# A spectral mixer and SwiGLU kernel: x loaded ahead of the filter, imaginary filter products first, and a later start for part of the second block

## The chip, the cores and the metric

The kernel runs on one core of one Trainium2 chip. A core has TensorE (PE, matmuls into PSUM; its weight loads are listed as PEld), VectorE (DVE), ScalarE (ACT), GpSimd (POOL) and SyncE (SP), which here issues transfers only. SP and POOL each issue DMA transfers into a queue of their own (q1 for SP, q0 for POOL in the profile); 16 DMA engines carry both. The metric is device time in microseconds, lower is better.

## The reference

The input x has 8 batches of 3008 rows of 256 channels. Each batch is filtered along its rows by a product in the frequency domain; then every row goes through an RMS norm and a gated feed-forward layer.

```
X = np.fft.rfft(x, axis=1)                     # x: (8, 3008, 256)
Y = X * (filt_r + 1j * filt_i)[None, :, :]     # filter: (1505, 256)
y = np.fft.irfft(Y, n=3008, axis=1).reshape(24064, 256)
rms = np.sqrt(np.mean(y * y, axis=-1, keepdims=True) + 1e-06)
xn = y / rms * rms_g
g = xn @ w_gate                                # (256, 1536)
out = (g / (1 + np.exp(-g)) * (xn @ w_val)) @ w_out   # (1536, 256)
```

## The kernel before

A batch is called a block. Its Fourier transform of length 3008 = 47 x 64 is done in two steps by matrix tables. `wa` transforms over 64 points, `wb` over 47 (with twiddles, one 96-column table for each of 32 values k2), `wi` and `wai` go back. All four tables, and two identity matrices (`ident` in fp16, `idf` in fp32) for turning tiles on PE, come from constants in HBM. Activations are kept in fp16, PSUM sums in fp32.

The steps of a block, with the function and its line in the profile:

- `x_load` (L188): a block's x comes in four groups (`xc`, 393 KB each as written), issued by POOL, which casts to fp16.
- `a0_unit` (L359) for block 0, `a_unit` (L208) for the others: the 64-point step on PE, then a copy from PSUM by ACT or DVE. Block 0 is turned on PE (`tr0_unit`, L369) with eight DVE copies into the tiles `t2`. The other blocks write `t1` to HBM (`z_store`, L213) and read it back turned (`t2_load`, L223).
- `b_unit` (L243) and `s_part` (L233 for e = 0, L236 for e = 1): the 47-point step for four k2 and one half of the channels; 16 units a block. From one PSUM bank DVE makes two products with the filter table `ff`: e = 0 with the real part, e = 1 with the negated and plain imaginary part. In block 0 both are summed and turned on PE (`yt0_unit`, L420).
- `bi_unit` (L287): back over 47 points; the result is copied into `uu`.
- `t4_load` (L301): SP turns `uu` by four DMA transposes into `t4`. In block 0, `t4_first` (L436) turns the first four row groups on PE, so that they need not wait for the DMA.
- norm: `first_norm` (L448 to L472) and `n_first`, `q_unit`, `scale_split`, `scale_apply` (L485 to L526) make `xn` for the first two row groups of block 0; `n_unit` and its followers make the rest.
- feed-forward: `gv` (L548 on PE, Silu at L552 on ACT, product at L553 on DVE) and `down` (L565). A block has 6 row groups m of 12 column tiles jt; each (m, jt) is a slot, 576 slots in all.

The filter: `f_load` (L384) brings filter rows in fp32, in six quarters of 512 KB (three row pieces i, f = 0 imaginary, f = 1 real), `f_unit` (L391) turns one with four PE transposes, and ACT writes it with two copies into `ff`. `f_neg` (L411) on POOL writes the negated imaginary part, `f_last` (L407) two edge columns.

The weights: `w_load` (L596) stages w_gate and w_val in fp32, `w_gain` (L608) on POOL multiplies by the gain of the norm, and `wo_load` (L600) brings w_out in three thirds of four jt each.

The order is written out by hand up to the first slot, and each engine runs its instructions in that order. `fill` (L428) issues matmuls whose result nobody reads. In the front, SP issues `idf`, the first imaginary quarter, `wa`, `ident`, `wai` and three single rows; POOL issues block 0's four x groups, five filter quarters, `wb` in halves, `wi`, the staged weights, and later block 1's x. A POOL DMA reuses one of eight semaphores and so waits for the DMA that used it eight issues earlier.

After that a planner gives each unit of later blocks a slot: `at(slot, fn, ...)` fixes one, `fit` looks for the first slot whose PSUM bank (M or B) is free and where ACT or DVE have room. `a_plan`, `b_plan` and `norm_plan` use it. In slot i PE gets `gv(i)`, then the planned units, then `down(i - 2)`.

Of the kernel before, what the change touches and what calls it, by code (L numbers as in the profile page):

```python
# [10 lines left out]
FP32 = mybir.dt.float32  # L11
FP16 = mybir.dt.float16
# [8 lines left out]
P = 128  # L21
D = 256
B = 8
# [15 lines left out]
def _make_tables():  # L39
    n2 = np.arange(N2)  # L40
    wa = np.zeros((P, P))
    wai = np.zeros((P, P))
    for h in range(2):
        r = slice(h, P, 2)
        for k2 in range(K2):
            c = np.cos(2 * np.pi * ((n2 * k2) % N2) / N2)
            s = np.sin(2 * np.pi * ((n2 * k2) % N2) / N2)
            re = 4 * k2 + 2 * h
            wa[r, re] = c
            wai[re, r] = c * (1.0 if k2 == 0 else 2.0)  # L50
# [12 lines left out]
    for k2 in range(K2):  # L63
        for q in range(SL):
            if q < H:
                k = k2 + 64 * q
                sign = 1.0
            else:
                j = q - H + 1
                k = 64 * j - (k2 if k2 else 32)  # L70
                sign = -1.0
                if j == H and k2:
                    continue
            th = 2 * np.pi * ((n1 * k) % N) / N
            c, sn = np.cos(th), np.sin(th)
            if k == 0 or k == NF - 1:
                sn = np.zeros(N1)
            if k2:
                wb[re, k2, q] = c
                wb[im, k2, q] = sign * sn  # L80
                wb[re, k2, SL + q] = -sn
                wb[im, k2, SL + q] = sign * c
            else:
                part = re if q < H else im
                wb[part, k2, q] = c
                wb[part, k2, SL + q] = -sn
                m = 1.0 if k in (0, NF - 1) else 2.0
                wi0[q, part] = m * c
                wi0[SL + q, part] = -m * sn
    f = np.float16  # L90
    r = np.arange(KR)
    wi = np.zeros((P, K2, KR))
    wi[:KR] = wb[:KR].transpose(2, 1, 0)
    wi[:KR, 0, :] = wi0
    wi[:, :, (r % H) * NR + r // H] = wi * S_INV_B
    return (wa.astype(f), (wai * S_INV_A).astype(f), wb.astype(f), wi.astype(f), np.eye(P).astype(f),
            np.eye(P).astype(np.float32))


@with_exitstack  # L100
def kernel(
# [10 lines left out]
):  # L112
    nc = tc.nc

    wa_np, wai_np, wb_np, wi_np, id_np, if_np = _make_tables()
    wa_d = nc.inline_tensor(wa_np, name="wa_t").ap()
    wai_d = nc.inline_tensor(wai_np, name="wai_t").ap()
    wb_d = nc.inline_tensor(wb_np, name="wb_t").ap()
    wi_d = nc.inline_tensor(wi_np, name="wi_t").ap()
    id_d = nc.inline_tensor(id_np, name="id_t").ap()  # L120
    if_d = nc.inline_tensor(if_np, name="if_t").ap()

    z_d = nc.dram_tensor("z_tmp", (B, K2, KR, D), FP16, kind="Internal").ap()

# [20 lines left out]
    wa = glob.tile([P, P], FP16)  # L145
    wai = glob.tile([P, P], FP16)
    ident = glob.tile([P, P], FP16)
    idf = glob.tile([P, P], FP32)
# [13 lines left out]
    epsb = glob.tile([P, 1], FP32)  # L162
    warm = glob.tile([P, 4], FP32)
    mhalf = glob.tile([P, 4], FP32)

    st = {b: {"x": {}, "t1": {}, "t2": {}, "s": {}, "yt": {}, "t4": {}, "y": {}, "sq": {},
              "u": {}, "xn": {}} for b in range(B)}
# [21 lines left out]
        st[b]["x"][c] = t  # L189

    def bank(i, name):
        pool, tag = ((psM, "mx"), (psG, "pg"), (psV, "pv"), (psB, "mb"))[i]
        return pool.tile([P, 512], FP32, tag=tag, name=name)

    def copy(eng, out, in_, scale=None):
# [39 lines left out]
            f2 = fv[:, :, 0:2 * SL].rearrange("p k (r q) -> p k r q", r=2)  # L235
            eng.tensor_tensor(out=o, in0=ps[:, :, ::-1, :], in1=f2, op=ALU.mult)  # L236

    def b_unit(b, i, bk=3):
        g, dh = divmod(i, 2)
        ps = bank(bk, "psb")[:, 0:4 * KR]  # L240
        for k in range(4):
            kk = 4 * g + k
            nc.tensor.matmul(ps[:, ts(k, KR)], st[b]["t2"][kk // KC][:, kk % KC, ds(dh * P, P)],  # L243
                             wb[0:KR, kk, :], start=True, stop=True)
        s = [sp.tile([P, 4, KR], FP16, tag="s%d" % e, name="s%d" % e) for e in range(2)]
        st[b]["s"][i] = (ps.rearrange("p (k r q) -> p k r q", k=4, r=2), s)
        s_part(b, i, 0)

    def b_soft(b, i, v=None):
        g, dh = divmod(i, 2)  # L250
# [124 lines left out]
    fst = {}  # L375
    FR4 = 4

    def f_load(i, f, eng):
        if i not in fst:
            fst[i] = stg.tile([P, 2, FR4, D], FP32, tag="stg", name="fs")  # L380
        t = fst[i]
        row = FR4 * P * i if i < 2 else NF - 1 - FR4 * P
        for src in ((filt_i, filt_r)[f],):
            eng.dma_start(t[:, f].rearrange("p a d -> p (a d)"),  # L384
                                raw(src, row, [[FR4 * D, P], [1, FR4 * D]]))

    def f_unit(i, f, dh, e):
# [224 lines left out]
    with tc.manual_schedule():  # L612
# [2 lines left out]
        nc.scalar.activation(out=warm, in_=epsb.to_broadcast([P, 4]), func=AXT.Sqrt)  # L615
        for c in range(NXC):
            x_load(0, c)
        nc.sync.dma_start(idf, if_d)
        f_load(0, 0, nc.sync)
        nc.sync.dma_start(wa, wa_d)  # L620
        nc.sync.dma_start(ident, id_d)
        nc.sync.dma_start(wai, wai_d)
        tail = op.tile([P, 4, D], FP32, tag="o3", name="tail")
        for f, src in ((0, filt_i), (1, filt_r)):
            nc.sync.dma_start(tail[0:1, f, :], raw(src, NF - 1, [[D, 1], [1, D]]))
        nc.sync.dma_start(tail[0:2, 2, 0:P], moe_rms_g.rearrange("(a p) -> a p", p=P))
        f_load(0, 1, nc.gpsimd)
        for i in range(1, 3):
            for f in range(2):
                f_load(i, f, nc.gpsimd)  # L630
        for h in range(2):
            nc.gpsimd.dma_start(wb[:, ts(h, K2 // 2), :], wb_d[:, ts(h, K2 // 2), :])
        nc.gpsimd.dma_start(wi, wi_d)
        w_load(0)
        w_load(1)
# [10 lines left out]
                for dh in range(2):  # L646
                    a0_unit(gq, dh, E[dh], 1 + dh)

        fill(5)
        for dh in range(2):  # L650
            f_unit(0, 0, dh, "A")
        fill(2)
        a0(0)
        fill(3)
        a0(1, 2)
        psg = bank(3, "psg")
        for f in range(2):
# [3 lines left out]
        copy("V", ff.rearrange("p e k (s q) -> p e k s q", s=3)[:, :, 0, 1:3, SL - 1],  # L661
             psg[:, 0:4].rearrange("p (e s) -> p e s", e=2))
        copy("V", gsb, psg[:, 4:6])
        fill(2)
        a0(3)
        fill(4)
        a0(4, 5)
        for dh in range(2):
            f_unit(0, 1, dh, "A")
        todo = {g: (1, *divmod(g, 2)) for g in range(4)}  # L670
        todo[4], todo[6] = (2, 0, 0), (2, 1, 0)
        for g in range(8):
            tr0_unit(g, "V")
            if g in todo:
                f_unit(*todo[g], "A")
        f_unit(2, 0, 1, "A")
        f_neg(4, 4, (0,))
        f_neg(8, 8, (0,))
        f_neg(4, 4, (1,))
        f_neg(8, 8, (1,))  # L680
        UN = K2 // 2
        od = [2, 4, 3, 5, 6, 7, 0, 1] + list(range(8, UN))
        for p in range(UN + 3):
            if p < UN:
                b_unit(0, od[p], (0, 3)[p % 2])
                s_part(0, od[p], 1)
            if p == 0:
                f_unit(2, 1, 1, "A")
                f_last()
                f_neg(0, 4)  # L690
                w_load(2)
                wo_load(0)
                f_neg(16, 16)
                wo_load(1)
                wo_load(2)
                for c in range(NXC):
                    x_load(1, c)
                for q in range(3):
                    w_gain(q)
            if p < 2:  # L700
                fill(2, 2)
            if 2 <= p < UN + 1:
                yt0_unit(od[p - 2], "A", 1)
            if p == UN + 1:
                yt0_unit(UN - 1, "V", 1, slice(0, 2))
                yt0_unit(UN - 1, "A", 0, slice(2, 4))
            if 4 <= p < UN + 3:
                bi_unit(0, od[p - 4], "AV"[p == UN + 1], 2)
            if UN + 1 <= p < UN + 3:
                fill(1, 1)  # L710
        bi_unit(0, UN - 1, "V", 3, slice(0, 2))
        bi_unit(0, UN - 1, "A", 0, slice(2, 4))
        t4_first()
        fill(2)
        for c in range(NXC):
            t4_load(0, c)
        first_norm()

        items = [(b, m, jt) for b in range(B) for m in range(6) for jt in range(JT)]
# [40 lines left out]
                at(s + d, fn, b, m)  # L760
            assert s + r[-1] + 1 < 72 * b + 12 * m

        XAT = {2: (5, 8, 11, 29), 3: (47, 51, 79, 88), 4: (112, 122, 132, 142)}

        def a_plan(b, slots):
            for i in range(12):
                opts = []
                for k in "MB":
                    opts.append((k, "A", ((k, 0, 1), ("A", 0, 0.6))))
# [41 lines left out]
        for b in range(1, B):  # L811
# [74 lines left out]
```

## Time and profile before

| | |
|---|---|
| median of 3 runs | 865.69 us (865.57 to 866.22) |
| the profiled execution | 865.26 us |
| its span, first to last instruction | 863.5 us |
| granted TensorE clock | 0.999 |
| first gate matmul of slot 0 | 43.91 us |
| first gate matmul of slot 10 | 60.39 us |

The span is the time between the first and the last instruction of the core; the execution has 1.8 us more around it. Times in the timelines are counted from the start of the span. "Idle before" is the time in which the engine waited, with what released it.

### The profile page before, as it was taken

How to read it: one execution, taken by the hardware profiler on the slowest of the kernel's cores; microseconds unless marked ns; L12 is line 12 of the kernel's file. 1: busy time of each engine (PE TensorE's matmuls, PEld its weight loads, DVE VectorE, ACT ScalarE, POOL GpSimd, SP SyncE). 2: the span in 40 equal slices, each digit the busy share in tenths (PEclk: the TensorE clock that was granted, in tenths of full speed). 3: DMA queues.
4: the chain of work that ended last, by engine and by line, in shares of the span. 5: the costliest groups of instructions: out<-in, count | busy, mean ns of one | idle time of the engine just before them, and what ended most of it. 6: DMA issues, size and time to landing. Idle time of an engine off the chain costs nothing.

```text
span 863.5 us, 17023 instructions
## 1 busy us (share of the span) xinstructions
PE 852.5 (99%) x6142; PEld 533.2 (62%) x6142; DVE 556.9 (64%) x925; ACT 613.7 (71%) x1340; POOL 296.8 (34%) x344
## 2 busy tenths in 40 slices
PE   8999999999999999999999999999999999999997
PEld 6755666566665666666666666666666666665664
DVE  4857655776666666666666676667666666555554
ACT  5887787777578756887578866888567765777443
POOL 5814841453144321534034430444123430132000
PEclk9999999999999999999999999999999999999999
DMA  9996688775975566646655658433564331521101
GB/s 283 279 179 138 135 168 167 129 137 124 196 146 120 132 150 110 148 110 143 136 127 115 130 103 173 115 87 95 136 127 93 94 72 42 125 53 49 62 25 50
DMA packets 198621, 107.98 MB, mean 125 GB/s; under 512 B 158982, under 2 KB 182920, under 8 KB 198536
## 3 DMA queue, kind: packets, MB, share of 16 engines
q1 hardware_dynamic: 190040, 86.04, 44.4%
q0 software_dynamic: 8352, 20.71, 12.4%
q8 instruction: 48, 0.79, 0.4%
q14 instruction: 37, 0.30, 0.1%
q10 hardware_dynamic: 144, 0.13, 0.0%
HBM read 45.78 MB, written 35.65 MB: 94 GB/s over the span
## 4 chain that ended last, share of the span: by engine, by line
PE 95%; DMA 2%; DVE 1%; ACT 1%; SPq 0%; issue 0%
PE po L565 28%; PE pg L548 28%; PE pv L548 28%; PE psb L243 3%; PE psi L287 2%; PE psn L316 2%; PE psa L208 2%; DMA tail<-in_moe_rms_g_dram 1%; DMA t<-uu 1%; PE psy L420 1%; PE psf L391 0%; PE pst L369 0%; DVE s L233 0%; DVE s L236 0%; DVE hh L553 0%
## 5 line engine op out<-in xcount | busy, mean ns | idle before, releaser
L553 DVE TENSOR_TENSOR hh<-pv,sg 128x512 f16<-128x512 f32 (+2 forms) x578 | 391.7, 678 | 287.3 <-ACT sg L552 222.2
L552 ACT ACTIVATE sg<-pg 128x512 f16<-128x512 f32 (+2 forms) x578 | 337.8, 585 | 216.7 <-PE pg L548 212.4
L548 PE MATMUL pg<-xn,wg 128*128 128x512 f16 (+2 forms) x1156 | 337.9, 374 | 0.0
L548 PE MATMUL pv<-xn,wv 128*128 128x512 f16 (+2 forms) x1156 | 337.8, 374 | 0.0
L565 PE MATMUL po<-wo,hh 128*128 128x256 f16 x2256 | 332.6, 272 | 0.0
L565 PEld LDWEIGHTS <-hh 128*128 128x128 f16 x2256 | 213.5, 98 | 105.3 <-issue 0.6
L270 POOL TENSOR_TENSOR ss<-s,s 128x384 f16<-128x384 f16 x112 | 102.0, 911 | 273.0 <-DVE s L236 245.3
L548 PEld LDWEIGHTS <-wv 128*128 128x128 f16 x1156 | 113.0, 98 | 130.6
L548 PEld LDWEIGHTS <-wg 128*128 128x128 f16 x1156 | 111.5, 98 | 16.9 <-issue 0.2
L342 POOL TENSOR_TENSOR xt<-y,rho 128x1024 f16<-128x1024 f32 (+1 forms) x46 | 85.4, 1857 | 2.9
L324 ACT ACTIVATE junk<-y 128x256 f16<-128x256 f32 x180 | 74.3, 413 | 2.8
L233 DVE TENSOR_TENSOR s<-psb,ff 128x384 f16<-128x384 f32 x124 | 67.8, 547 | 0.0
L236 DVE TENSOR_TENSOR s<-psb,ff 128x384 f16<-128x384 f32 x124 | 67.8, 547 | 0.0
L197 ACT ACTIVATE uu<-psi 128x384 f16<-128x384 f32 (+1 forms) x127 | 61.7, 486 | 1.5 <-PE psb L243 0.5
L197 ACT ACTIVATE y<-psn 128x512 f32<-128x512 f32 (+1 forms) x95 | 55.8, 588 | 4.2
L287 PEld LDWEIGHTS <-yt 96*128 96x128 f16 x512 | 35.4, 97 | 26.7 <-issue 1.0
L334 POOL TENSOR_TENSOR rho<-u,mhalf 128x4 f32<-128x4 f32 (+1 forms) x46 | 46.5, 1010 | 3.8
L332 POOL TENSOR_SCALAR u<-ss 128x4 f32<-128x4 f32 (+1 forms) x46 | 8.9, 194 | 104.3 <-ACT junk L324 103.3
L197 ACT ACTIVATE t<-psa 128x512 f16<-128x512 f32 x71 | 42.0, 595 | 3.2 <-PE psa L208 1.7
L287 PE MATMUL psi<-wi,yt 96*128 96x96 f16 x512 | 42.9, 205 | 0.1
L243 PE MATMUL psb<-wb,t 96*128 96x96 f16 x480 | 40.2, 206 | 0.5 <-DVE s L236 0.3
L243 PEld LDWEIGHTS <-t 96*128 96x128 f16 x480 | 28.7, 97 | 13.8 <-DVE s L236 3.9
(98 smaller groups left out, 366.1 us busy)
## 6 DMA issues: line engine op xcount, KB each, us to landing
out_dram<-o SPq DMA_DIRECT2D x40, 512.0 KB, 3.6
xc<-in_x_dram POOLq DMA_DIRECT2D x31, 384.0 KB, 6.0
z_tmp<-t SPq DMA_DIRECT2D x28, 384.0 KB, 2.6
t<-z_tmp SPq DMA_DIRECT2D x28, 384.0 KB, 6.1
out_dram<-o SPq DMA_DIRECT2D x7, 384.0 KB, 2.7
fs<-in_filt_r_dram POOLq DMA_DIRECT2D x3, 512.0 KB, 12.1
ws<-in_moe_w_gate_dram POOLq DMA_DIRECT2D x3, 512.0 KB, 11.5
ws<-in_moe_w_val_dram POOLq DMA_DIRECT2D x3, 512.0 KB, 11.7
```

The source lines that it names most:

```text
L197: nc.scalar.activation(out=out, in_=in_, func=AXT.Copy, **({} if scale is None else {"scale": scale}))
L233: eng.tensor_tensor(out=o, in0=ps, in1=f1, op=ALU.mult)
L236: eng.tensor_tensor(out=o, in0=ps[:, :, ::-1, :], in1=f2, op=ALU.mult)
L243: nc.tensor.matmul(ps[:, ts(k, KR)], st[b]["t2"][kk // KC][:, kk % KC, ds(dh * P, P)], wb[0:KR, kk, :], start=True, stop=True)
L270: nc.gpsimd.tensor_tensor(out=ss3[g % 3][:, :, dh, 0:KR], in0=s[0], in1=s[1], op=ALU.add)
L287: nc.tensor.matmul(ps[:, k, :], yt[0:KR, k, dh, :], wi[0:KR, 4 * g + k, :], start=True, stop=True)
L324: nc.scalar.activation(out=junk, in_=y[:, i, ts(u, D)], func=AXT.Square, accum_out=ss[:, 2 * i + u:2 * i + u + 1])
L342: nc.gpsimd.tensor_tensor(out=xt[:, 0:n, :], in0=y.rearrange("p a (u d) -> p (a u) d", u=2)[:, 0:n, :], in1=rho[:, 0:n].unsqueeze(2).to_br ...
L548: nc.tensor.matmul(ps[:, 0:w], wt[:, dt_, ts(jt, P)], xn[:, q0:q1, dt_, :], start=(dt_ == 0), stop=(dt_ == 1))
L552: nc.scalar.activation(out=sg[:, c], in_=pg[:, 0:w], func=AXT.Silu)
L553: nc.vector.tensor_tensor(out=hh[:, c], in0=pv[:, 0:w], in1=sg[:, c], op=ALU.mult)
L565: nc.tensor.matmul(po[s4 // 2][:, s4 % 2, :], hh[:, ts(s4, P)], wo[:, jt, :], start=(jt == 0 and s4 % 2 == 0), stop=(jt == JT - 1 and (s4 ...
```

## The change

Tables: `wa`, `wai`, `ident` and `idf` become one constant `tab` with rows of 1,280 bytes, loaded by one DMA from SP.

Loads: all six filter quarters are issued by POOL, after block 0's x. A piece of `wb` (k2 4 to 15) is loaded before the last real quarter, the rest after it.

Fillers: ten before the first x products instead of five; four, three and four later; none in the spectrum loop's first two rounds, one in place of two behind the first turning. Before the norm there are 24 as before.

Filter units and spectrum: two filter units that stood ahead of the x products now follow them. `b_unit` takes the part e to do first. The order of spectrum units starts 2, 4, 6 in place of 2, 4, 3; the first three do their imaginary products first, and their real products follow once the last real quarter's unit has been issued. The third uses a PSUM bank of the output sums.

Block 1: two of its projections (`a_unit` 0 and 1) are done around `t4_first`; the third group of w_out and the fourth x group are issued by POOL behind a small copy `seen` that reads the second turned group. `n_first` for the second row group of block 0, and what follows it, move one slot later.

```diff
@@ tables @@
-    return (wa.astype(f), (wai * S_INV_A).astype(f), wb.astype(f), wi.astype(f), np.eye(P).astype(f),
-            np.eye(P).astype(np.float32))
+    tab = np.concatenate([wa.astype(f), (wai * S_INV_A).astype(f), np.eye(P).astype(f),
+                          np.eye(P).astype(np.float32).view(f)], axis=1)
+    return tab, wb.astype(f), wi.astype(f)
...
+    tab = glob.tile([P, 5 * P], FP16)
+    wa, wai, ident = (tab[:, ts(i, P)] for i in range(3))
+    idf = tab[:, 3 * P:5 * P].bitcast(FP32)
...
+    seen = glob.tile([P, 4], FP16)
...
-        pool, tag = ((psM, "mx"), (psG, "pg"), (psV, "pv"), (psB, "mb"))[i]
+        pool, tag = ((psM, "mx"), (psG, "pg"), (psV, "pv"), (psB, "mb"), (psO, "po0"))[i]
...
-    def b_unit(b, i, bk=3):
+    def b_unit(b, i, bk=3, e=0):
...
-        s_part(b, i, 0)
+        s_part(b, i, e)
@@ loads @@
-        nc.sync.dma_start(idf, if_d)
-        f_load(0, 0, nc.sync)
-        nc.sync.dma_start(wa, wa_d)
-        nc.sync.dma_start(ident, id_d)
-        nc.sync.dma_start(wai, wai_d)
+        nc.sync.dma_start(tab, tab_d)
...
-        f_load(0, 1, nc.gpsimd)
-        for i in range(1, 3):
-            for f in range(2):
-                f_load(i, f, nc.gpsimd)
-        for h in range(2):
-            nc.gpsimd.dma_start(wb[:, ts(h, K2 // 2), :], wb_d[:, ts(h, K2 // 2), :])
+        for n in range(6):
+            if n == 5:
+                nc.gpsimd.dma_start(wb[:, 4:16, :], wb_d[:, 4:16, :])
+            f_load(*divmod(n, 2))
+        nc.gpsimd.dma_start(wb[:, 16:K2, :], wb_d[:, 16:K2, :])
+        nc.gpsimd.dma_start(wb[:, 0:4, :], wb_d[:, 0:4, :])
@@ x products and fillers @@
-        fill(5)
-        for dh in range(2):
-            f_unit(0, 0, dh, "A")
-        fill(2)
+        fill(10)
         a0(0)
-        fill(3)
+        fill(4)
         a0(1, 2)
...
-        fill(2)
+        fill(3)
         a0(3)
         fill(4)
         a0(4, 5)
@@ filter units and spectrum @@
-        for dh in range(2):
-            f_unit(0, 1, dh, "A")
-        todo = {g: (1, *divmod(g, 2)) for g in range(4)}
-        todo[4], todo[6] = (2, 0, 0), (2, 1, 0)
-        for g in range(8):
+        todo = [(i, f, dh) for i in range(2) for f in range(2) for dh in range(2)][:7] + [(2, 0, 0)]
+        for u in todo[0:2]:
+            f_unit(*u, "A")
+        for g in range(7):
             tr0_unit(g, "V")
-            if g in todo:
-                f_unit(*todo[g], "A")
-        f_unit(2, 0, 1, "A")
+            if g < 6:
+                f_unit(*todo[g + 2], "A")
         f_neg(4, 4, (0,))
         f_neg(8, 8, (0,))
-        f_neg(4, 4, (1,))
-        f_neg(8, 8, (1,))
         UN = K2 // 2
-        od = [2, 4, 3, 5, 6, 7, 0, 1] + list(range(8, UN))
+        od = [2, 4, 6, 3, 5, 7, 0, 1] + list(range(8, UN))
+        tr0_unit(7, "V")
+        for p in range(2):
+            b_unit(0, od[p], (0, 3)[p], 1)
+        f_unit(1, 1, 1, "A")
+        f_unit(2, 0, 1, "A")
+        b_unit(0, od[2], 4, 1)
+        f_unit(2, 1, 0, "A")
+        for p in range(3):
+            s_part(0, od[p], 0)
         for p in range(UN + 3):
-            if p < UN:
+            if 3 <= p < UN:
                 b_unit(0, od[p], (0, 3)[p % 2])
                 s_part(0, od[p], 1)
             if p == 0:
                 f_unit(2, 1, 1, "A")
+                f_neg(4, 12, (1,))
                 f_last()
                 f_neg(0, 4)
                 w_load(2)
                 wo_load(0)
                 f_neg(16, 16)
                 wo_load(1)
-                wo_load(2)
-                for c in range(NXC):
+                for c in range(3):
                     x_load(1, c)
                 for q in range(3):
                     w_gain(q)
-            if p < 2:
-                fill(2, 2)
@@ around the first turning @@
+        a_unit(1, 0, "A", 1)
         t4_first()
-        fill(2)
+        a_unit(1, 1, "V", 0)
+        fill(1, 3)
         for c in range(NXC):
             t4_load(0, c)
+        nc.gpsimd.tensor_copy(out=seen, in_=st[0]["t4"][1][:, 0, 0:4])
+        wo_load(2)
+        x_load(1, 3)
         first_norm()
@@ the plan @@
-        XAT = {2: (5, 8, 11, 29), 3: (47, 51, 79, 88), 4: (112, 122, 132, 142)}
+        XAT = {2: (6, 8, 11, 29), 3: (47, 51, 79, 88), 4: (112, 122, 132, 142)}
...
-            for i in range(12):
+            for i in range(2 * (b == 1), 12):
...
-        at(2, n_first, 1)
-        at(4, q_unit, 1)
-        at(6, scale_split, 1)
-        at(8, scale_apply, 1, 3)
-        load["M"][2] = load["M"][3] = 1
-        load["B"][2] = load["B"][3] = load["B"][4] = load["B"][8] = load["B"][9] = 1
-        load["A"][2] = load["A"][3] = 1.2
+        at(3, n_first, 1)
+        at(5, q_unit, 1)
+        at(7, scale_split, 1)
+        at(9, scale_apply, 1, 3)
+        load["M"][3] = load["M"][4] = 1
+        load["B"][3] = load["B"][4] = load["B"][5] = load["B"][9] = load["B"][10] = 1
+        load["A"][3] = load["A"][4] = 1.2
```

More of the change, by code (lines that the diff above doesn't have):

```diff
@@ L113 @@
     nc = tc.nc
-    wa_np, wai_np, wb_np, wi_np, id_np, if_np = _make_tables()
-    wa_d = nc.inline_tensor(wa_np, name="wa_t").ap()
-    wai_d = nc.inline_tensor(wai_np, name="wai_t").ap()
+    tab_np, wb_np, wi_np = _make_tables()
+    tab_d = nc.inline_tensor(tab_np, name="tab_t").ap()
     wb_d = nc.inline_tensor(wb_np, name="wb_t").ap()
     wi_d = nc.inline_tensor(wi_np, name="wi_t").ap()
-    id_d = nc.inline_tensor(id_np, name="id_t").ap()
-    if_d = nc.inline_tensor(if_np, name="if_t").ap()
     z_d = nc.dram_tensor("z_tmp", (B, K2, KR, D), FP16, kind="Internal").ap()
@@ L143 @@
     psB = ctx.enter_context(tc.tile_pool(name="psB", bufs=1, space=bass.MemoryType.PSUM))
[L145 to L148, printed above, removed]
+    tab = glob.tile([P, 5 * P], FP16)
+    wa, wai, ident = (tab[:, ts(i, P)] for i in range(3))
+    idf = tab[:, 3 * P:5 * P].bitcast(FP32)
     wb = glob.tile([P, K2, KR], FP16)
@@ L244, in b_unit @@
                              wb[0:KR, kk, :], start=True, stop=True)
-        s = [sp.tile([P, 4, KR], FP16, tag="s%d" % e, name="s%d" % e) for e in range(2)]
+        s = [sp.tile([P, 4, KR], FP16, tag="s%d" % n, name="s%d" % n) for n in range(2)]
         st[b]["s"][i] = (ps.rearrange("p (k r q) -> p k r q", k=4, r=2), s)
-        s_part(b, i, 0)
+        s_part(b, i, e)
     def b_soft(b, i, v=None):
@@ L376, with f_load @@
     FR4 = 4
-    def f_load(i, f, eng):
+    def f_load(i, f):
         if i not in fst:
@@ L383, in f_load @@
         for src in ((filt_i, filt_r)[f],):
-            eng.dma_start(t[:, f].rearrange("p a d -> p (a d)"),
+            nc.gpsimd.dma_start(t[:, f].rearrange("p a d -> p (a d)"),
                                 raw(src, row, [[FR4 * D, P], [1, FR4 * D]]))
```

## The prediction

> **What bounds the kernel now.** First the page's busy table and chain, to see which engine sets the end.
>
> ```profile
> PE 852.5 (99%) x6142; PEld 533.2 (62%) x6142; DVE 556.9 (64%) x925; ACT 613.7 (71%) x1340; POOL 296.8 (34%) x344
> ...
> PE 95%; DMA 2%; DVE 1%; ACT 1%; SPq 0%; issue 0%
> ```
>
> TensorE (PE) is 95% of the chain, so time is won only where PE waits or drops work. Next PE's waits (total us, times, longest) and the busy time of one early stage (length, then PE, PEld, DVE, ACT, POOL).
>
> ```profile
> PE psf L391 <- DMA fs<-in_filt_i_dram: 1.3, 1, 1.3
> PE psg L660 <- DMA tail<-in_moe_rms_g_dram: 0.8, 1, 0.8
> PE psn L485 <- DMA t<-uu: 0.7, 1, 0.7
> ...
> 22.50:37.60 15.10, 14.80 (x242) 12.64 (x240) 15.04 (x33) 13.43 (x31) 14.59 (x25) 1.00 1.15 302
> ```
>
> Up to 43.9 us, where the first gate matmul starts, PE is not the bound, though fillers keep it busy. From 22.5 to 37.6 VectorE (DVE) works 15.04 of 15.10 us: 32 products at L233 and L236, 15.0/32 = 0.47 us each. So the question for the front is when the first product starts. The timelines of PE, DVE and POOL tell (start, length, engine, line, instruction, count, idle before and releaser):
>
> ```profile
> 13.28 1.06 PE L359 MATMUL psa<-wa,xc 128*128 128x128 f16 x16
> 14.43 1.07 PE L391 MATMUL psf<-idf,fs 128*128 128x128 f32 x8
> 15.34 0.61 PE L369 MATMUL pst<-ident,uu 128*96 128x128 f16 x8
> ...
> 21.11 1.41 DVE L199 COPY t2o<-pst 96x1024 f16<-96x1024 f16 x2
> 22.51 0.56 DVE L233 TENSOR_TENSOR s<-psb,ff 128x384 f16<-128x384 f32 x1
> ...
> 36.99 0.54 DVE L236 TENSOR_TENSOR s<-psb,ff 128x384 f16<-128x384 f32 x1
> ...
> 7.30 0.53 POOL L384 DMA_DIRECT2D fs<-in_filt_r_dram  x1 [1.26 <-DMA xc<-in_x_dram]
> ...
> 13.31 0.53 POOL L633 DMA_DIRECT2D wi<-wi_t  x1 [1.36 <-DMA xc<-in_x_dram]
> 14.58 0.74 POOL L596 DMA_DIRECT2D ws<-in_moe_w_gate_dram  x1 [0.74 <-DMA fs<-in_filt_r_dram]
> 15.85 0.73 POOL L596 DMA_DIRECT2D ws<-in_moe_w_val_dram  x1 [0.53 <-DMA fs<-in_filt_i_dram]
> ```
>
> POOL's issues wait for old slots, so its releases read off landings: the first x group by 7.3, the fourth by 13.3, then a filter quarter each 1.27 us. Transfers land one behind another; the DMA share is 9 in the first slices. PE's last x products (13.28) follow the fourth group.
>
> **The change, part by part.** The sum is made against the profiled execution: 865.26 us, span 863.5. The median shown, 865.69, lies 0.43 above it, and differences are carried over to it.
>
> *x first.* The first imaginary quarter leaves SP's queue and goes to POOL's, behind four x groups. Of an x group issued into an idle queue the trace has two: 4.7 us to landing at 53.4, 4.5 at 93.3. Issued at 1.25, the first group should land near 6.0 instead of 7.0 (1.25 plus 5.8). Block 1's groups land 1.87 us apart (38.5 for the one issued at 30.13, 44.1 for the one at 31.79), so the fourth lands at 6.0 + 5.6 = 11.7 instead of 13.0: 1.3 us gained. Bounds: the first lands 5.8 at best (1.25 + 4.5) and 7.0 if its start does not move; I take the idle-queue row, since only the filter quarter stood before it. Merging four tables into one takes 96 KB of 256-byte rows out of the x stream (the second landed 7.2 us after its issue), worth 0.1 to 0.15 us per group, already in the 1.87.
>
> *The filter behind x.* Quarters land at 13.0, 14.3, 15.5, 16.8 and 18.1. The 288 KB piece of the wb table costs 0.75 (by size from quarters of 512 KB in 1.27), so the last real quarter lands at 20.2, against 19.4 before (7.3 plus 12.1). One slow engine can make it 21.6: the first wb half took 12.5 us, landing 1.5 later than its size asks.
>
> *PE, ScalarE (ACT) and DVE up to the first product.* PE ends x products 1.3 earlier, at 12.8. Two filter units that used to run before x at 5.11 now stand at 13.1 (the quarter's landing), just as two others stood at 14.43. So the first turning of va (15.34) comes at 14.0, and the row of eight copies, one per 0.89 us while filter units alternate with them, ends at 21.2 instead of 22.5. Three imaginary products then need only imaginary filter and f_neg on POOL (0.84 for the two, behind ACT's copies of unit (2,0,0) at 20.1, so 21.0): hidden under the DVE copies. The real products need filter unit (2,1,0). It is the third of three filter units behind the last turning (20.3 on PE, 0.17 for each spectrum unit between); ACT takes 0.64 us for each pair of copies from 21.1 on, so they end near 23.1, and DVE, done with three products at 22.6, waits 0.5. From 23.1 come 29 products at 0.47: last end 36.7 instead of 37.5. **Gain 0.8**; 0.1 to 1.2 by the bounds on x and on the last quarter, whose landing PE needs at 21.8.
>
> *The two projections ahead.* On PE a_unit(1,0), 0.22 us, goes into the 0.2 that PE waits for ACT before the first turning at 39.37, and (1,1) replaces one of the two fillers (0.22 each) behind it. The loop's four fillers move to the start, where PE waits for x. a_unit(1,0)'s copy, 0.6 on ACT, goes into a 0.68 us hole before t4f; (1,1)'s 0.69 on DVE into 1.12 us before y. Without these holes each costs its length. New wait: PE stops at a_unit(1,0) until block 1's first x group has landed, with the turning, the norm and all gates behind it. That group landed at 38.5; one third of the output weights now waits behind it (1.3 by the spacing of such thirds, issued 28.6 and 29.4 and landing 35.3 and 36.6), so 37.2, and PE comes at 38.3. Hidden by 1.1; beyond, each us late costs one. So 6.4 us from the last product to the first gate remain.
>
> *Held weights and x group.* POOL waits in the small copy `seen` for the second turned group; behind it stand a third of wo (first used in slot 10), x group 3 (slot 9) and the power at q_unit. The x queue then ends at 40.9 instead of 44.1, and the second turned group, 4.1 us behind the last x in the old trace (48.2), lands near 45.0. Released then, those transfers land by 52; slot 9 starts near 57. Cost nothing.
>
> *Block 1's second norm a slot later.* PE's instruction lists of both kernels are equal from slot 10 on. Slots 0 to 9 took 43.91 to 60.39, with ten projections; now eight. One of the two sat in a hole behind ACT's first Silu, so dropping both saves 0.22. The wait for the turned group goes:
>
> ```profile
> 48.24 0.40 PE L485 MATMUL psn<-wai,t 128*128 128x128 f16 x4 [0.74 <-DMA t<-uu]
> ...
> 49.17 1.08 ACT L197 ACTIVATE y<-psn 128x512 f32<-128x512 f32 x2
> ```
>
> n_first now starts about 47.5, after 45.0. Its four ACT instructions, 2.1 us, delay slot 4's Silu to 50.5; its buffer is asked for by slot 6 at 51.4, so nothing new waits. **Gain 0.95**, 0.2 if that margin fails.
>
> Sum: 0.8 + 0.95 = 1.75. Span 861.75, execution 863.5, **863.9** on the median's scale. The terms' ends together give 0.3 to 2.2.
>
> **The rivals.**
>
> *A, x starts no sooner.* Between 2.6 and 4.05 us the DMA view has packets of SP's queue alone; x may simply not have been ready. For A: later two queues do share engines (59 to 60 us: 44 and 46 packets). Against: the z store issued at 55.56 also shows no packet from 56.4 to 57.2, while 52 of x's run; a newcomer waited out the transfer in flight.
>
> ```profile
> q1 hardware_dynamic: 104, 0.43, 78.3%
> ...
> q0 software_dynamic: 52, 0.16, 101.9%
> ```
>
> Then the fourth x group lands at 12.6 and the first quarter at 13.9; the copies end at 22.1, and behind three products (1.4) and the 0.5 hole come 29 more, ending at 37.6 against 37.5. So 865.69 - 0.95 + 0.1 = 864.8.
> The Trainium skill bears on A: "DMA: Bandwidth & Descriptors", section "Queues, rings and completion order", says each engine goes round-robin between the queues that have work. By that rule a ready x would have mixed with the filter quarter, so A's 864.8 would follow; the 55.56 row disagrees with it, the 59 to 60 row agrees.
>
> *B, ACT takes the DMA's place.* If ACT's 2.1 us of n_first hold slot 6, PE's 0.74 returns: 864.7. For it: DVE idled 2.59 behind ACT at 48 to 51 even before. Against: the margin of 0.9 above.
>
> *C, slower.* PE waits at a_unit(1,0). It begins at a landing of 38.3, eats the whole gain at 40.1, and passes 0.2% at 41.8. At 42.1, where the third group used to land, it costs 3.8: 867.7. For: that landing hangs on everything queued before it, and on POOL reaching the load behind the 16-row negation. Against: 1.1 us of margin, and the load was issued 8.4 before landing, so POOL is early.
>
> *D, more.* If x lands at best and the last quarter releases DVE without its 0.5 hole, 863.3.
>
> **How the numbers follow.** My forecast (863.4 to 864.4) gets 0.60, A 0.14, B 0.11, C 0.10, D 0.05. This kernel's measurement tells 0.2%, 1.73 us, from no change, which is 863.96: just above the forecast. Of the 0.60 I put 0.49 on the faster side, as the x bounds lean to more; with D and 0.03 of B, faster is 0.57. A, the rest of B (0.08) and 0.11 of the forecast make 0.33 the same; C makes 0.10 slower. The range runs from 862.9, a little beyond D, to 865.2, above A; C is left out.
>
> **What would show it.** Right: POOL's first release from x near 6.0; va's first turning near 14.0; first product (now L234) near 21.2, last near 36.7; first gate near 43.1; no wait for t<-uu at n_first (now L483); slot 10 at 58.6. A shows as x by 7 again; B as PE holes before slot 6; C as PE waiting for xc at L206. Wrong altogether: a difference arising after slot 10.

## The result, and the profile after

| | before | after | difference |
|---|---|---|---|
| median | 865.66 us (864.78 to 866.22, 8 runs) | 863.19 us (863.0 to 863.43, 8 runs) | -2.47 |
| ratio, 95% interval | | 0.9973 [0.9962, 0.9984] | |
| profiled execution | 865.26 | 863.15 | -2.11 |
| span | 863.5 | 861.4 | -2.1 |
| first turning of va | 15.34 | 13.93 | -1.41 |
| first product of the spectrum | 22.51 | 21.20 | -1.31 |
| end of the last product | 37.54 | 37.01 | -0.53 |
| first gate matmul of slot 0 | 43.91 | 43.38 | -0.53 |
| first gate matmul of slot 10 | 60.39 | 58.65 | -1.74 |
| end of the last matmul | 858.34 | 856.57 | -1.77 |

The kernel is faster by 0.27%; its median lies 0.7 us below the forecast 863.9. The rows show where: 0.53 us up to the first gate, 1.21 us in slots 0 to 9, and next to nothing after that; from slot 10 to the last matmul it is 797.95 us before and 797.92 after. The remaining 0.34 of the profiled difference lies behind the last matmul, in the last stores.

PE's busy table, chain and waits after. The wait for the turned group (0.7 us before) is gone from the list. One wait of 0.8 us has come in, at L418: PE waits there for DVE's first real products, in the stretch in which DVE and not PE sets the pace:

```profile
PE 852.4 (99%) x6142; PEld 532.2 (62%) x6142; DVE 557.2 (65%) x926; ACT 612.4 (71%) x1339; POOL 297.8 (35%) x346
...
PE 96%; DMA 1%; ACT 1%; DVE 1%; issue 0%; POOL 0%; POOLq 0%
...
PE psy L418 <- DVE s L231: 0.8, 1, 0.8
PE psf L389 <- DMA fs<-in_filt_i_dram: 0.4, 1, 0.4
```

The two stretches that changed, as windows (length, then busy PE, PEld, DVE, ACT, POOL). The first runs from the first product to just behind the last, the second over slots 0 to 9:

```profile
21.20:37.10 15.90, 14.87 (x242) 13.06 (x240) 15.12 (x33) 14.69 (x35) 14.11 (x24) 1.00 1.11 315
43.38:58.65 15.27, 15.15 (x110) 9.29 (x109) 8.12 (x17) 12.25 (x24) 4.38 (x7) 1.00 0.97 180
```

and slots 0 to 9 of the kernel before:

```profile
43.91:60.39 16.48, 15.74 (x112) 9.43 (x111) 9.09 (x18) 13.41 (x26) 2.83 (x4) 1.00 0.93 172
```

DVE works 15.12 of 15.90 us in the first stretch, where it worked 15.04 of 15.10 before: it now idles for 0.78 us. In the second PE has 0.12 us of idle time left of 0.74, and two matmuls fewer.

The timelines of after, first POOL, whose releases show when x landed (start, length, engine, line, instruction, count, idle before and releaser):

```profile
6.30 0.53 POOL L382 DMA_DIRECT2D fs<-in_filt_i_dram  x1 [0.26 <-DMA xc<-in_x_dram]
...
11.91 0.54 POOL L625 DMA_DIRECT2D wb<-wb_t  x1 [1.31 <-DMA xc<-in_x_dram]
13.18 0.54 POOL L626 DMA_DIRECT2D wb<-wb_t  x1 [0.73 <-DMA fs<-in_filt_i_dram]
...
46.02 0.18 POOL L713 COPY seen<-t 128x4 f16<-128x4 f16 x1 [6.64 <-DMA t<-uu]
```

The first x group is there by 6.3 instead of 7.3, the fourth by 11.9 instead of 13.3. The landing records of the trace say 6.02 and 11.63, and 45.97 for the turned group that `seen` reads. Then PE, DVE and ACT:

```profile
13.03 1.06 PE L389 MATMUL psf<-tab,fs 128*128 128x128 f32 x8 [0.40 <-DMA fs<-in_filt_i_dram]
13.93 0.61 PE L367 MATMUL pst<-tab,uu 128*96 128x128 f16 x8
...
38.48 0.38 PE L206 MATMUL psa<-xc,tab 128*128 128x512 f16 x1
...
47.80 0.61 PE L483 MATMUL psn<-tab,t 128*128 128x128 f16 x8
...
51.71 0.59 PE L546 MATMUL pg<-xn,wg 128*128 128x512 f16 x2
```

```profile
19.99 1.28 DVE L197 COPY t2o<-pst 96x1024 f16<-96x1024 f16 x2 [0.20 <-PE pst L367]
21.20 1.47 DVE L234 TENSOR_TENSOR s<-psb,ff 128x384 f16<-128x384 f32 x3
23.31 2.10 DVE L231 TENSOR_TENSOR s<-psb,ff 128x384 f16<-128x384 f32 x4 [0.64 <-ACT ff L195]
```

```profile
49.25 1.10 ACT L195 ACTIVATE y<-psn 128x512 f32<-128x512 f32 x2
50.20 1.12 ACT L550 ACTIVATE sg<-pg 128x512 f16<-128x512 f32 x2
```

The three imaginary products follow the last copy without a gap; then DVE idles 0.64 us for ACT, which is writing the real filter. The projection at 38.48 and `n_first` at 47.80 wait for nothing.

### The profile page after: what moved, and what is told of

The parts are those of the page before. It is cut to its first block, busy times and chain, and to the rows that moved or that the text cites. A ratio compares the mean times of both kernels' runs of the same rounds, so it can differ in the third digit from the quotient of the medians.

```text
span 861.4 us, 17024 instructions
## 1 busy us (share of the span) xinstructions
PE 852.4 (99%) x6142; PEld 532.2 (62%) x6142; DVE 557.2 (65%) x926; ACT 612.4 (71%) x1339; POOL 297.8 (35%) x346
## 3 DMA queue, kind: packets, MB, share of 16 engines
q0 software_dynamic: 8544, 21.24, 12.7%
## 4 chain that ended last, share of the span: by engine, by line
PE 96%; DMA 1%; ACT 1%; DVE 1%; issue 0%; POOL 0%; POOLq 0%
PE po L563 28%; PE pg L546 28%; PE pv L546 28%; PE psb L241 3%; PE psi L285 3%; PE psn L314 2%; PE psa L206 2%; DMA fs<-in_filt_i_dram 1%; PE psy L418 1%; PE psf L389 1%; PE pst L367 0%; ACT sg L550 0%; POOL xc L186 0%; DVE s L231 0%; DVE hh L551 0%
```

## The experiments

All kernels compute the whole output. Each is the changed kernel with the edit shown. Markers are read from PE's and DVE's timelines, in us; "slots" is from the first gate of slot 0 to that of slot 10.

| kernel | time | first turning | first product | last product ends | first gate | slots |
|---|---|---|---|---|---|---|
| before | 865.26 | 15.34 | 22.51 | 37.54 | 43.91 | 16.48 |
| after | 863.15 | 13.93 | 21.20 | 37.01 | 43.38 | 15.27 |
| quarter_ahead_of_x | 864.3 | 15.10 | 22.31 | 38.13 | 44.50 | 15.27 |
| real_first | 864.19 | 13.94 | 22.95 | 38.05 | 44.42 | 15.27 |
| real_quarter_sooner | 862.87 | 13.85 | 21.57 | 36.68 | 43.05 | 15.27 |
| third_projection_slot0 | 862.86 | 13.83 | 21.10 | 36.92 | 43.29 | 15.05 |
| no_hold | 863.2 | 14.02 | 21.29 | 37.11 | 43.48 | 15.27 |
| slot_back | 863.22 | 13.98 | 21.52 | 37.06 | 43.43 | 15.27 |
| no_hold_slot_back | 864.94 | 14.14 | 21.41 | 37.23 | 43.60 | 16.80 |
| projections_planned | 863.66 | 14.14 | 21.41 | 37.23 | 43.60 | 15.49 |
| late_x | 867.25 | 13.91 | 21.18 | 37.00 | 47.43 | 15.27 |
| both_improved | 862.35 | 13.82 | 21.09 | 36.49 | 42.86 | 15.05 |
| neg_ahead | 862.57 | 13.76 | 21.03 | 36.59 | 42.96 | 15.05 |
| after_again | 863.09 | 13.84 | 21.11 | 36.92 | 43.29 | 15.27 |

Times are of the profiled execution. In every one of these kernels the way from slot 10 to the last matmul is 797.92 to 797.98, so the two columns on the right hold an edit's effect up to the last matmul. The first turning of the same front varies by 0.4 us between executions (13.76 to 14.14); what follows it is best read as a difference from it.

### Is x really first? (quarter_ahead_of_x)

```diff
         nc.sync.dma_start(tab, tab_d)
+        f_load(0, 0, nc.sync)
...
-        for n in range(6):
+        for n in range(1, 6):
```

> The changed kernel with one edit undone: the first imaginary filter quarter goes back to SP's queue, ahead of x; the order on the engines stays. Theory (x first frees the transfer engines for x): the first x group lands near 7.0 instead of 6.0 and the fourth near 12.7 instead of 11.6; the first turning of va starts near 14.8 instead of 13.9, and the first gate matmul near 44.2 instead of 43.4. Rival A (x could not have started sooner anyway): x lands as in the changed kernel, and the first gate stays at 43.4 or comes earlier.

POOL's releases again:

```profile
7.80 0.55 POOL L624 DMA_DIRECT2D wb<-wb_t  x1 [1.76 <-DMA xc<-in_x_dram]
9.72 0.53 POOL L382 DMA_DIRECT2D fs<-in_filt_r_dram  x1 [1.37 <-DMA xc<-in_x_dram]
```

The first x group lands at 7.52 by the landing records instead of 6.02, the fourth at 13.10, the first gate comes 1.12 later. So x was ready and kept back by the quarter: rival A is refuted. The packets show how it was kept back. x was issued at 1.25 in both kernels. Between 2.75 and 3.75 us the queue of x (q0) has packets in after, and in quarter_ahead_of_x the quarter's queue (q1) alone has them; after first:

```profile
q0 software_dynamic: 29, 0.09, 110.0%
```

```profile
q1 hardware_dynamic: 98, 0.40, 103.2%
```

x waited the quarter out. The rule of the Trainium skill that the prediction set beside A ("DMA: Bandwidth & Descriptors", section "Queues, rings and completion order") is round-robin between the queues that have work. By it a ready x would have had packets beside the quarter, which is why A's 864.8 followed from it; here a ready x had none.

### Are the imaginary products worth being first? (real_first)

```diff
-        for p in range(2):
-            b_unit(0, od[p], (0, 3)[p], 1)
         f_unit(1, 1, 1, "A")
         f_unit(2, 0, 1, "A")
-        b_unit(0, od[2], 4, 1)
         f_unit(2, 1, 0, "A")
         for p in range(3):
-            s_part(0, od[p], 0)
+            b_unit(0, od[p], (0, 3, 4)[p])
+        for p in range(3):
+            s_part(0, od[p], 1)
```

> The changed kernel with the first three spectrum units done real product first, so their matmuls and products stand behind the unit of the last real filter quarter. Theory (the imaginary products fill the time until the last real quarter is in the table): DVE stands idle from 21.2 to about 23.3, 2.1 us in place of 0.64, and the first gate comes 1.4 later, near 44.8. Rival (the order does not matter, ACT's chain sets the loop): less than 0.3 later.

DVE's timeline of this kernel:

```profile
20.00 1.28 DVE L197 COPY t2o<-pst 96x1024 f16<-96x1024 f16 x2 [0.20 <-PE pst L367]
22.95 1.49 DVE L231 TENSOR_TENSOR s<-psb,ff 128x384 f16<-128x384 f32 x3 [1.67 <-ACT ff L195]
```

DVE idles 1.67 us in one piece in place of 0.64 between the products, and the first gate is 1.04 later. Both are less than expected (2.1 and 1.4), since the real filter came 0.36 us sooner here: the first real product starts at 22.95, in after at 23.31. At 44.42 this front is half a microsecond behind that of the kernel before, though its copies are done 1.2 us sooner: with the filter behind x the real quarter comes late, and x first pays only when there is work that can do without it.

### The hole, mended (real_quarter_sooner)

```diff
-        f_unit(2, 0, 1, "A")
         b_unit(0, od[2], 4, 1)
         f_unit(2, 1, 0, "A")
+        f_unit(2, 0, 1, "A")
```

> The changed kernel with filter unit (2,1,0) issued one place earlier, ahead of (2,0,1). Theory (the 0.64 us that DVE waits before its first real product is ACT's order of filter copies): the first real product starts near 22.7 instead of 23.3, the last product ends near 36.4 instead of 37.0, the first gate comes near 42.8. Rival 1 (the last real quarter's landing, 21.2, sets it): the wait shrinks by less than 0.3. Rival 2 (the wait moves to the fourth unit's imaginary product, whose negated filter part comes later): a hole of 0.3 or more appears there and the gate gains under 0.3.

The gate came 0.33 sooner, less than expected. DVE and POOL of this kernel:

```profile
21.57 1.50 DVE L234 TENSOR_TENSOR s<-psb,ff 128x384 f16<-128x384 f32 x3 [0.38 <-POOL ff L409]
22.98 2.09 DVE L231 TENSOR_TENSOR s<-psb,ff 128x384 f16<-128x384 f32 x4
```

```profile
20.33 0.72 POOL L594 DMA_DIRECT2D ws<-in_moe_w_val_dram  x1 [1.13 <-DMA wb<-wb_t]
21.17 0.84 POOL L409 TENSOR_SCALAR ff<-ff 128x192 f32<-128x192 f32 x2
```

The first real product starts at 22.98 instead of 23.31, and the hole before it is gone, but in part only because the first product of all started 0.37 late. It waited for POOL's negation, and POOL stood for 1.13 us in a load that reuses the semaphore of the wb piece. Of that piece's sixteen parts the first landed at 18.27 and the last at 20.05; in after all had landed by 18.77. `slot_back` shows the same late product (21.52), there swallowed by the hole.

### The third projection in slot 0 (third_projection_slot0)

```diff
-                z = a_plan(b, [i for i in range(12)])
+                z = a_plan(b, [0 if i == 2 else i for i in range(12)])
```

> The changed kernel with the third projection of block 1 planned into slot 0 instead of slot 2. Theory (PE has a hole of 0.35 us between slot 0 and slot 1 behind ACT's first Silu): the projection is free there, the way from the first gate of slot 0 to that of slot 10 shrinks by 0.2, from 15.27 to about 15.05. Rival (its copy on ACT delays the Silu of slot 1 and with it slot 2 or 3): 15.2 or more.

Slots 15.05, by 0.22 less: the projection went into the hole behind the first Silu, which the two projections taken out of the plan had left free.

### The hold and the later slot, one by one and together

no_hold:

```diff
+                wo_load(2)
-                for c in range(3):
+                for c in range(NXC):
                     x_load(1, c)
...
-        nc.gpsimd.tensor_copy(out=seen, in_=st[0]["t4"][1][:, 0, 0:4])
-        wo_load(2)
-        x_load(1, 3)
```

slot_back (no_hold_slot_back has both edits):

```diff
-        at(3, n_first, 1)
-        at(5, q_unit, 1)
-        at(7, scale_split, 1)
-        at(9, scale_apply, 1, 3)
+        at(2, n_first, 1)
+        at(4, q_unit, 1)
+        at(6, scale_split, 1)
+        at(8, scale_apply, 1, 3)
```

> The changed kernel without the hold: the last third of the output weights and the fourth x group of block 1 are issued where they were before, n_first stays in slot 3. Theory (the hold and the later slot each suffice): the second turned group lands near 47.7 instead of 46.0, n_first's second half comes at 48.0, so PE waits 0 to 0.1 and slot 10 stays within 0.15 of 58.65. Rival (the hold is what removes the wait): PE waits 0.3 or more for the turned group.

> The changed kernel with n_first, q_unit and the scale back in slots 2, 4, 6 and 8, the hold kept. Theory (either suffices): the turned group lands near 46.0, n_first's second half comes near 46.5, no wait, slot 10 within 0.15 of 58.65. Rival (the later slot is what removes the wait): PE waits 0.3 or more at n_first.

> The changed kernel with both undone: no hold, and n_first back in slot 2. Theory: the wait is back, about 1.1 us (landing near 47.7 against 46.6), and slot 10 comes 1.0 to 1.2 later, near 59.75. If the way to slot 10 is no longer than in the changed kernel, neither of the two edits did anything and the two projections alone made the gain there.

Undone alone, neither costs anything: slots 15.27 both times. The hold does bring the turned group forward. SP's four transposes end sooner with it; after first, then no_hold:

```profile
39.05 8.11 SPq L299 DMA_TRANSPOSE t<-uu  x4
```

```profile
39.15 10.10 SPq L299 DMA_TRANSPOSE t<-uu  x4
```

The second group lands at 45.97 with the hold and at 47.97 without. It is the second half of `n_first` that needs it, some 0.22 behind the start. In no_hold `n_first` starts at 47.90, so its second half comes at 48.12, 0.15 behind the landing; in slot_back it starts at 46.34 and the second half comes at 46.56, 0.5 behind its own landing (46.03). With both undone PE waits twice:

```profile
47.09 0.40 PE L483 MATMUL psn<-tab,t 128*128 128x128 f16 x4 [0.42 <-DMA t<-uu]
...
48.26 0.40 PE L483 MATMUL psn<-tab,t 128*128 128x128 f16 x4 [0.77 <-DMA t<-uu]
```

and the slots take 1.53 longer (1.0 to 1.2 expected), even longer than before. So the hold and the later slot are two remedies for one wait; either is enough in these executions, the later slot alone with a margin of 0.15 us and the hold alone with one of 0.5, and together they leave 2.1.

### The two projections, back in the plan (projections_planned)

```diff
-        a_unit(1, 0, "A", 1)
         t4_first()
-        a_unit(1, 1, "V", 0)
-        fill(1, 3)
+        fill(2)
...
-            for i in range(2 * (b == 1), 12):
+            for i in range(12):
```

> The changed kernel with the first two projections of block 1 given back to the planner (slots 0 and 1) and the second filler behind the first turning put back. Theory (one of the two hides behind ACT's first Silu): the first gate stays at 43.4, slot 10 comes 0.2 to 0.25 later. Rival (both are on PE's path in the slots): 0.43 later. Second rival (they cost something around the turning): the first gate comes earlier by 0.1 or more.

Slots 0 to 9 of this kernel as a window:

```profile
43.60:59.09 15.49, 15.49 (x112) 9.50 (x110) 8.12 (x17) 13.15 (x26) 4.39 (x7) 1.00 0.94 175
```

15.49 against 15.27: the two projections are worth the 0.22 of the prediction, and the front they were moved into paid nothing (from the first turning to the first gate 29.46 here, 29.45 in after). With the same 112 matmuls as before the stretch is 0.99 shorter, so the wait that went was worth 0.99, not the 0.74 listed as its idle time (the section on the prediction adds it up).

### Rival C made true (late_x)

```diff
-                for c in range(3):
-                    x_load(1, c)
                 for q in range(3):
                     w_gain(q)
+                for c in range(3):
+                    x_load(1, c)
```

> The changed kernel with block 1's first three x groups issued behind the twelve gain multiplications on POOL, near 39.1 instead of 29.3. Price of rival C: PE stops in order at the projection ahead of the first turning (38.5) until the first group lands, near 43.8 (4.7 us behind its issue), so the first gate comes 5.3 later, near 48.7, and nothing later makes it up: the execution takes 5 to 5.5 us longer. Rival (fillers and the norm's waits behind it absorb part): under 4 us longer.

The first x group of block 1 was issued at 37.34 and not at 39.1, and so it landed at 41.82 and not at 43.8. PE of this kernel:

```profile
41.87 0.40 PE L206 MATMUL psa<-xc,tab 128*128 128x512 f16 x1 [3.24 <-DMA xc<-in_x_dram]
...
43.34 0.63 PE L426 MATMUL pf<-ss 128*128 128x512 f16 x1
```

and the same filler in after:

```profile
39.71 0.38 PE L426 MATMUL pf<-ss 128*128 128x512 f16 x1
```

The first gate is 4.05 later and the execution 4.1: slower than before, though by less than the 5 to 5.5 expected, since x landed sooner. Of the 4.05, 3.39 is the wait from start to start (41.87 against 38.48 in after; the idle column lists 3.24, the rest is hidden in the row before). The other 0.66 is PE after the wait, 5.56 us from the projection to the gate in place of 4.90. One 512-column filler takes 0.63 in place of 0.38 until about 45, then 0.47 and less. The granted clock (the third number from the right in a window) falls to half for just this stretch:

```profile
38.60:42.12 3.52, 0.28 (x3) 0.14 (x3) 0.34 (x1) 0.40 (x2) 0.86 (x2) 1.00 1.03 166
42.12:45.53 3.41, 3.41 (x25) 2.19 (x23) 1.58 (x3) 2.29 (x5) 0.00 (x0) 0.50 1.05 186
45.53:47.43 1.90, 1.74 (x12) 0.99 (x12) 1.48 (x5) 1.56 (x4) 0.00 (x0) 1.00 1.26 256
```

Over the whole span it is 0.998, as 3.41 us at half are lost in 865. The Trainium skill, "TensorE: Matmul & The Clock Gate", Part 1, says that an idle window of about 3.4 us puts PE on half its clock until it has been busy as long; the trace agrees in the size (0.50) and the length (3.41 us), and an idle time listed as 3.24 us was enough for it.

### The improvements together (both_improved, neg_ahead, after_again)

both_improved has the edits of real_quarter_sooner and third_projection_slot0. neg_ahead adds this, which lets POOL do the negation before the load that can wait:

```diff
         w_load(0)
-        w_load(1)
...
         f_neg(4, 4, (0,))
         f_neg(8, 8, (0,))
+        w_load(1)
```

after_again is the changed kernel once more, on the same chip as neg_ahead.

> The changed kernel with two edits: filter unit (2,1,0) one place earlier, and the third projection in slot 0. If both gains are real and independent they add: first gate near 42.8, way from slot 0 to slot 10 near 15.05, 0.8 us less than the changed kernel, about 3.2 us less than the kernel before (ratio 0.9963). If one of them only moves a wait, 0.2 or 0.6 less than the changed kernel.

> Both improvements of the run before (the last real quarter's unit one place sooner, the third projection of block 1 in slot 0), and POOL issues the two negations for the first products ahead of the staged w_val load instead of behind it. My theory: POOL's negation then waits for ScalarE's copy alone, never for the semaphore of the wb piece that sometimes lands a microsecond late. The first product starts near 21.1 whatever that piece does (it began at 21.57 in the run with the quarter sooner, 21.09 with both), the first gate comes at 42.8 to 42.9, slots 0 to 10 take 15.05, slot 10 starts at 57.9, the execution takes 862.3. Rival: the staged load, issued some 1.0 us later, reaches w_gain too late, or the negation runs into another wait; then the gate is at 43.1 or later, or PE waits at the first value matmuls, and it is no better than the kernel without this.

> The changed kernel as it is, beside the run before it on one chip, so that the three small improvements are measured against it: 863.2 (first product 21.2, first gate 43.4, slot 10 at 58.65), 0.9 above the kernel with the three. Rival: the profile's gain of 0.7 to 0.8 at slot 10 is not there in the times, and both have the same median within 0.3.

| kernel | median | before on that chip | ratio, 95% interval |
|---|---|---|---|
| both_improved | 862.56 (862.22 to 862.87, 6 runs) | 865.38 (864.82 to 866.15) | 0.9968 [0.9956, 0.9981] |
| neg_ahead | 862.57 (862.29 to 862.74, 5 runs) | 865.75 (864.97 to 867.86) | 0.996 [0.9946, 0.9973] |
| after_again | 863.26 (863.07 to 864.52, 7 runs) | 865.75 (864.97 to 867.86) | 0.997 [0.996, 0.9981] |

The profiled execution of both_improved is 0.80 us below that of after, as expected; after was not run on its chip. Against before, its median gained 2.8 of the 3.2 expected. neg_ahead beats both before and after: on the chip that it shares with after_again its slowest run, 862.74, is below the fastest of after_again, 863.07, and the medians are 0.69 apart (0.9 expected). The profile gives 0.55 at slot 10 (0.33 at the first gate, 0.22 in the slots). POOL and DVE of neg_ahead:

```profile
20.10 0.84 POOL L409 TENSOR_SCALAR ff<-ff 128x192 f32<-128x192 f32 x2 [2.52 <-ACT ff L195]
20.89 0.77 POOL L594 DMA_DIRECT2D ws<-in_moe_w_gate_dram  x1
```

```profile
21.03 1.47 DVE L234 TENSOR_TENSOR s<-psb,ff 128x384 f16<-128x384 f32 x3
22.88 1.49 DVE L231 TENSOR_TENSOR s<-psb,ff 128x384 f16<-128x384 f32 x3 [0.38 <-ACT ff L195]
```

The wb piece was late in this execution too (20.26), as in real_quarter_sooner, and the first product started on time all the same: the semaphore was the cause of the late start there. Against both_improved, where the piece came early (18.66), nothing is gained (0.1 later at the gate). The hole that is left, 0.38 here and 0.21 there, follows the last real quarter: it landed at 21.42 and 21.31, and PE turned its first unit at 21.55 and 21.45.

## Why the prediction was right, point by point

**x first: held.** 11.7 was forecast for the fourth group and 11.63 came; 14.0 for the first turning and 13.93 came; 21.2 for the first product and 21.20 came. quarter_ahead_of_x shows the cause.

**From the first product to the last: the step that was mis-sized.** The prediction had "DVE, done with three products at 22.6, waits 0.5. From 23.1 come 29 products at 0.47: last end 36.7." The first real product came at 23.31 and the last ended at 37.01, so the front gained 0.53 instead of 0.8. ACT began its copies at 21.24 instead of 21.1, and then did not run through as the sum assumed: it stood 0.22 us before the third pair, the real one, because PE turned the real unit only at 21.95. By the order of rows PE could have started it at 21.64 (four spectrum matmuls from 21.47 on, 0.17). What held it was its first weight load (PEld), which waited for ACT; ACT's row, and PEld's waits between 21 and 23 us:

```profile
22.64 1.16 ACT L195 ACTIVATE ff<-psf 128x256 f32<-128x256 f32 x4 [0.22 <-PE psf L389]
...
PEld psf L389 <- ACT ff L195: 0.3, 1, 0.3
```

The filter units write into a pool of two PSUM tiles, so the third unit needs the tile of the first, and ACT's second copy out of that one ended at 21.90. The prediction had no term for this. The row "0.64 idle" also understates the hole: start to start it is 0.71, since a DVE row's length runs past the next start. That the order of the units and not the load held the real products back in after is shown by real_quarter_sooner, in which the first of them starts 0.33 sooner although the quarter landed at 21.32 instead of 21.24; with that done the quarter's landing is the limit.

**6.4 us to the first gate: held**, 6.37 in both.

**Projections ahead: held**, 0.22 (projections_planned). PE came to the first at 38.48 and its x was there at 36.80; 38.3 and 37.2 were forecast.

**Held weights and x: held at no cost.** The third of the output weights landed at 52.2 and the x group at 55.1, against 52 for both; slot 9 and slot 10 did not wait. The turned group came at 45.97, a microsecond later than forecast, which the later slot covered.

**The wait at `n_first`: right, but worth 0.99 instead of 0.74.** That is why slots 0 to 9 gained 1.21 and not 0.95. I had taken the idle column as the price. Counted from start to start, the 0.99 is all there. In the kernel before the two halves of `n_first` start 1.13 us apart, where a half takes 0.22 without a wait: 0.91. And the first half starts 0.51 behind the value matmuls, where 0.43 is usual: 0.08 more, a wait for the first turned group (landed at 47.06) that is short enough to be hidden in the length of the row before it:

```profile
46.60 0.59 PE L548 MATMUL pv<-xn,wv 128*128 128x512 f16 x2
47.11 0.40 PE L485 MATMUL psn<-wai,t 128*128 128x128 f16 x4
```

no_hold_slot_back says the same: 0.42 and 0.77 are listed there, 1.19 in all, and the slots take 1.53 longer.

**The sum.** The two errors, 0.27 too much and 0.26 too little, cancelled by luck: 1.75 forecast, 1.74 measured at slot 10. That the median came 0.7 below the forecast has two further sources. The last stores ended 0.33 sooner in the profiled execution (4.81 us from the last matmul to the end of the span against 5.14; the other kernels have 4.67 to 4.83, so the profile of before was the odd one). And I carried the 0.43 by which the median of before lies above its profiled execution over to after, where the median is only 0.04 above its own. Where the runs of before lose that time is open, as only one of them has a profile. They spread over 1.44 us, those of after over 0.43; the wait for the turned group, which before has and after has not, may differ from run to run, but that is not shown.

**The rivals.** A is refuted above. B did not come: slot 4's Silu started at 50.20 (50.5 forecast) and slot 6's gate followed without a wait. C did not come, by a margin of 1.7 us, and its price was too low, as late_x shows: the wait cost one for one, and its 3.4 us then halved the clock for another 3.4. Of D's conditions neither was met: the first x group landed at 6.02, not at 5.8, and the hole was there.

One point stays open: no run separates the merged tables, the fillers or the split of `wb` from the rest of the front.

## What to carry to other kernels

Bringing the first input forward pays only as far as the next one that is needed; here x first is worth 1.1 us, but only since imaginary products could run while the real filter was still coming. Price a removed wait from start to start of the instructions, not by the idle column. And when one late transfer can be covered in two ways (release it sooner, use it later), try each alone: here either was enough, and a wait on an engine's queue ahead of unrelated work (POOL's load ahead of its negation) is worth moving even if it waits only in some executions.

## What the runs showed of the hardware that was not expected

- One of the sixteen parts of a transfer can be late by far more than its size asks. In after the parts of the last real quarter landed from 19.65 to 21.24, and the loads behind it show the same spread of 1.5 to 1.6 us, where those ahead of it have 0.4. A 16 KB instruction load of 1.1 us goes with it. In the twelve profiles whose loads up to the last real quarter come in the order of after, it starts between 17.8 and 18.6 us. In the three in which it had started by 18.05 the wb piece is already late (landed at 20.0 to 20.3); in the nine in which it started at 18.07 or later the wb piece landed by 19.0 and the quarter behind it is the first to be late (21.2 to 21.5). That the instruction load is the cause is likely by this, but no run moves it.
- Through the reuse of semaphores such a lag reaches an engine that has no use for the data: POOL waited 1.13 us for the wb piece ahead of a negation that needed ACT alone.
- A transfer issued from POOL's queue had no packets while SP's 512 KB quarter ran (none against 98 from 2.75 to 3.75 us), though the same load had 29 in that time when the quarter was out of its way.
- PE ran on half its clock for 3.41 us after 3.24 us of listed idle time, at a cost of 0.66 us. The granted clock of the whole span, 0.998, hides that; the granted clock of a short window shows it (0.50).
